# Spectral filter tail spread into block form by one masked VectorE product per block, with three copies moved to ScalarE and a new order of the filter stage

## The chip, the cores and the metric

The kernel runs on one core of a Trainium2 chip. The metric is the device time of one execution in microseconds (us); the profile's span is about 1.9 us shorter, because it runs from the first to the last instruction. Before the change the median was 494.26 us in three runs (493.99 to 494.33). All runs quoted here were in the fast state, with a granted TensorE clock of 1.0 (0.997 in one run of e5).

## The reference

Two layers over 2048 tokens of width 576: a spectral filter (two-dimensional real FFT, product with a learned complex filter, inverse FFT), then a gated feed-forward layer of width 4608, each after a layer norm and each added to its input.

```python
def _A_ref(x, w_r, w_i):
    X = jnp.fft.rfft2(x.astype(jnp.float32), axes=(-2, -1))
    return jnp.fft.irfft2(X * (w_r + 1j * w_i), s=(S, D), axes=(-2, -1)).astype(jnp.bfloat16)
def _B_ref(x, w_gate, w_up, w_down):
    return (_gelu(x @ w_gate) * (x @ w_up)) @ w_down
h  = x + _A_ref(_layernorm(x), A_w_r, A_w_i)
h2 = h + _B_ref(_layernorm(h), B_w_gate, B_w_up, B_w_down)
```

## The kernel before

The transforms are matmuls with tables. The middle of the first layer, the **filter stage**, works on 16 groups of frequencies and runs from about 20 to 51 us. Each group i passes through these steps, whose order is a hand-written list:

- D: matmuls into PSUM, copied to CUS; B: matmuls on CUS, copied to YS.
- T: VectorE multiplies YS by the filter weights WS (and their negated copy, made by the operations "w", the **flips**).
- Z: VectorE adds the halves: a wide part ZS (256 columns) and a narrow part ZR (the last 32 of 288 columns, the **tail**). Four groups share the 128 columns of one ZR block.
- V: matmuls on ZS, result copied to the array V. R: matmuls on a ZR block, result copied to VR.

The inverse transform then takes V and VR as 128-row operands. The four groups in a block of 128 rows must not mix, so VR is block-shaped: rows 32j to 32j+31 hold data only for group j and zeros for the other three. Before the change the zeros come from one fill and the data from one narrow copy per group. In the code, `P.op` records one operation of an engine with what it reads (r) and writes (w), `ev` a copy out of PSUM, and `bank(b, ...)` is a piece of PSUM bank b (abridged):

```python
def st_R(q, engs, b=7):
    # ... n = 32 columns per group of this block
    for zp in range(2):
        P.op(PE, lambda t, ...: t.matmul(bank(b, 0, n, 0, 256), ZR[:, q % 2, zp, 0:n], VT[:, sp_, zp, :], ...))
    for j, i in enumerate(js):
        ev(engs[j], VR[32*j:32*j+32, :, :, GORD[i], :]..., bank(b, 32*j, 32*j+32, 0, 256)..., [("PS", b), "Vz"], ...)

P.op(POOL, lambda g: g.memset(VR[:, :, :, :, :], 0.0), r=[("ATS", c) for c in range(NT)], w=["Vz"])
for w in SEQF:      # the order of the filter stage, a list of steps
    ...
```

`engs` says for each copy whether VectorE (DVE) or ScalarE (ACT) does it; another list, VENG, does so for the V copies. What follows is the inverse transform (I, N), the second norm and, from 62.34 us to the end, the feed-forward.

Of the kernel before, what the change touches and what calls it, by code (L numbers as in the profile page):

```python
# [5 lines left out]
F32 = mybir.dt.float32  # L6
ACTF = mybir.ActivationFunctionType
ALU = mybir.AluOpType
# [7 lines left out]
NT = 16  # L16
# [6 lines left out]
SEQ1 = """k14 B0 B1 v0 Q2 S2 B3 q0 v1 n0 n2 c0 q1 S4 x0D c1 M0 E1A B6 E0A Q4 B5 B7 x1P v2 E2D n1 B8 E3A E4A k104 M1 q2 c2 B9 Q10 E5A E7A n3 v3 S10 B12 E6A q3 c3 x2P B11 k202 M2 E9A x3P Q13 v4 E12A E8A q4 n4 B14 c4 B15 E10A E11A S13 E13D M3 E14A E15A v5 x4P E16D q5 E17A c5 E18A M4 n5 x5D E20D E19A E22D E21A M5 E23D E24A E25A E27A E26D E29A E28D""".split()  # L23
LORD = "x0-2 x2-4 a0-4 x4-8 a4-8 x8-12 x12-16 a8-16".split()
ACT_TILES = tuple(int(w[1:]) for w in SEQ1 if w[0] == "Q")
SEQF = """D0 w1 w0 D1 D2 B0 T0 B1 T1 Z1 D3 D4 B2 Z0 D5 T2 B3 T3 Z2 B4 T4 D6 B5 D7 Z3 B6 Z4 T5 T6 V0 V1 Z5 Z6 D8 R0 B7 D9 V2 T7 w3 D10 V3 Z7 w2 B8 T8 B9 V4 T9 Z9 B10 D11 R1 Z8 D12 T10 V5 D13 B11 Z10 B12 V6 D14 T11 T12 B13 Z11 V7 D15 Z12 T13 R2 B14 V8 Z13 B15 T14 V9 Z14 T15a V11 V12 T15b V10 V13 Z15a Z15b V14 V15 R4 R3""".split()
RENG = [['dve', 'dve', 'act', 'act'], ['act', 'dve', 'act', 'dve'], ['dve', 'dve', 'act', 'dve'], ['act', 'act', 'dve'], ['dve']]
VENG = [('act',), ('act',), ('act',), ('act',), ('act',), ('dve',), ('act',), ('act',), ('act',), ('act',), ('act',), ('act',), ('act',), ('act',), ('dve',), ('dve', 'act')]
DENG, BENG = ['act', 'dve', 'dve', 'act', 'act', 'act', 'act', 'act', 'act', 'act', 'act', 'act', 'act', 'act', 'act', 'act'], ['dve', 'act', 'act', 'act', 'act', 'act', 'act', 'act', 'act', 'act', 'act', 'act', 'act', 'act', 'act', 'act']
QR = ((0, 2), (2, 4), (4, NPRE), (NPRE, 16))  # L30
SEQ = """I0 I1 N0 I2 s0 N1 I3 N2 m0 s1 I4 r0 q0 s2 N3 c0 m1 s3 n1 n0 r1 I5 q1 N4 I6 A1 c1 n3 A0 n2 N5 I7 D2 z3 N6 N7""".split()
# [278 lines left out]
def _build(nc, A_x, A_w_r, A_w_i, B_w_gate, B_w_up, B_w_down, out):  # L310
    P = Prog(nc)
    T = build_tables()
    dram = {n: nc.inline_tensor(_np_bf16(T[n]), name="c_" + n.lower()) for n in T}
    PE, DVE, ACT, SP, POOL = "pe", "dve", "act", "sp", "pool"
# [3 lines left out]
    sb = SbufMap(nc, base, top)  # L318
# [11 lines left out]
    V = sb.alloc("V", [128, NT, 4, NG, 8], BF16)  # L330
    VR = sb.alloc("VR", [128, NT, 2, NG, 8], BF16)
# [22 lines left out]
    TM = sb.alloc("TM", [128, 2, NT], F32)  # L354
    RS2 = sb.alloc("RS2", [128, NT], F32)
    EPT = sb.alloc("EPT", [128, 1], F32)
    OS = sb.alloc("OS", [128, 2, D], BF16)
    shared = (sb.off + 63) // 64 * 64

# [12 lines left out]
    VT = sb.alloc("VT", [128, 2, 2, 256], BF16)  # L372
# [7 lines left out]
    ATS = sb.alloc("ATS", [128, NT, 128], BF16)  # L380
# [7 lines left out]
    ZR = sb.alloc("ZR", [128, 2, 2, 128], BF16)  # L388
# [8 lines left out]
    PS = nc.alloc_psum_tensor("PS", [128, 4096], F32)  # L397

    def bank(b, p0=0, p1=128, c0=0, c1=512):
        return PS[p0:p1, b * 512 + c0:b * 512 + c1]  # L400
# [4 lines left out]

    P.op(POOL, lambda g: g.memset(EPT[:, :], EPS), w=["EPT"])
    P.op(POOL, lambda g: g.memset(ZD[:, :], 0.0), w=["ZD"])
    xv = A_x[0].rearrange("(p c) d -> p c d", c=NT)
    ov = out[0].rearrange("(p c) d -> p c d", c=NT)
    tabs = dram["ATAB"].rearrange("p (c k) -> p c k", c=NT)  # L410
# [34 lines left out]
    GORD = list(range(1, NG)) + [0]  # L445
# [34 lines left out]
    def ln1_sqrt(i):  # L480
        c0, c1 = GROUPS[i]
        P.op(ACT, lambda a, c0=c0, c1=c1: a.activation(RS1[:, c0:c1], MV1[:, c0:c1, 1], ACTF.Sqrt, bias=EPT[:, 0:1]),
             r=[("MV1", c) for c in range(c0, c1)] + ["EPT"], w=[("SD1", i)])

# [56 lines left out]
    RUN1 = {"k": idle_mm, "S": act_sum, "Q": act_sq, "B": ln1_tile, "v": ln1_var, "q": ln1_sqrt, "c": ln1_rs, "M": a_mm, "x": ln1_scale, "E": a_ev, "n": x_neg}  # L541
    P.op(ACT, lambda a: a.activation(SA[:, 0, 0:1], EPT[:, 0:1], ACTF.Sqrt), r=["EPT"], w=[("SA0", 0)])
    for w in SEQ1:
        a = w[1:]
# [8 lines left out]
    FB, used = {}, [0] * 8  # L553
    for t, w in enumerate(SEQF):
        k, i = w[0], w[1:].rstrip("abc")
        if k in "DB":
            late = ("V", 0) in FB or any(x[0] == "V" for x in SEQF[t:t + 4])
            b = min((0, 2, 4) if late else (0, 2, 4, 6), key=lambda b: max(used[b], used[b + 1]))
            used[b] = used[b + 1] = t + 1
        elif k in "VR":  # L560
            b = min((6, 7) if ("D", LAST) not in FB else range(8), key=lambda b: used[b])
            used[b] = t + 1
            if k == "V":
                b2 = b
                if int(i) == LAST and len(VENG[LAST]) > 1:
                    b2 = min(range(8), key=lambda b: used[b])
                    used[b2] = t + 1
                b = (b, b2)
# [4 lines left out]
    def ev(eng, dst, src, r, w):  # L573
        fn = (lambda v: v.tensor_copy(dst, src)) if eng == DVE else (lambda a: a.activation(dst, src, ACTF.Copy))  # L574
        P.op(eng, fn, r=r, w=w)

    def st_D(i, eng=ACT):
        g = GORD[i]
        b0, s3 = FB["D", i], i % 3
        for o in range(2):  # L580
            b = b0 + o
            for m, us in enumerate((1 - o, 3 - o, 4) if o == 0 else (4, 1 - o, 3 - o)):
                P.op(PE, lambda t, b=b, m=m, us=us, o=o, g=g: t.matmul(bank(b, 0, 128, 0, 2 * HK), U[:, us, g, :, :], FT[:, 3 * o + (2 if us == 4 else us // 2), :], start=(m == 0), stop=(m == 2)),  # L583
                    r=uk[us] + ["FT"], w=[("PS", b)])
        ev(eng, CUS[:, s3, :, :].rearrange("p a (j r) -> p a j r", r=2), banks(b0, 2, 2 * HK).rearrange("p r (a j) -> p a j r", a=2),
           [("PS", b0), ("PS", b0 + 1)], [("CU", s3)])
# [18 lines left out]
    def st_w(i):  # L605
        for g0, g1 in (((1, 5),), ((5, 9),), ((9, 13),), ((13, 16), (0, 1)))[i]:
            P.op(DVE, lambda v, g0=g0, g1=g1: v.tensor_scalar(WS[:, 0, g0:g1, :], WS[:, 2, g0:g1, :], -1.0, None, op0=ALU.mult),  # L607
                 r=[k for k in (wkeys[0] if i < 2 else wkeys[1] if i < 3 else wkeys[0] + wkeys[1]) if k[2] == 1], w=[("Wn", 4 * i + k) for k in range(4)])
# [19 lines left out]
            ev(e, V[:, :, k0:k1, g, :].rearrange("p n k e -> p k n e"), bank(b[a], 0, 128, 128 * k0, 128 * k1).rearrange("p (k n e) -> p k n e", k=k1 - k0, n=16),  # L628
               [("PS", b[a])], [("V", g, k) for k in range(k0 // 2, k1 // 2)])

    def st_R(q, engs, b=7):
        js = [i for i in range(4 * q, 4 * q + 4) if i < LAST] if q < 4 else [LAST]
        sp_, n = (1, 32) if q == 4 else (0, 32 * len(js))
        for zp in range(2):
            P.op(PE, lambda t, b=b, zp=zp, n=n, q=q, sp_=sp_: t.matmul(bank(b, 0, n, 0, 256), ZR[:, q % 2, zp, 0:n], VT[:, sp_, zp, :], start=(zp == 0), stop=(zp == 1)),
                 r=[("ZR", q % 2, j) for j in range(len(js))] + ["VT"], w=[("PS", b)])
        for j, i in enumerate(js):
            ev(engs[j], VR[32 * j:32 * j + 32, :, :, GORD[i], :].rearrange("p n k e -> p k n e"), bank(b, 32 * j, 32 * j + 32, 0, 256).rearrange("p (k n e) -> p k n e", k=2, n=16),
               [("PS", b), "Vz"], [("V", GORD[i], 2)])

    def idle_ft(n, b):
        for _ in range(n):
            P.op(PE, lambda t, b=b: t.matmul(bank(b, 0, 128, 0, 2 * HK), FT[:, 0, 0:128], FT[:, 0, :], start=True, stop=True), r=["FT"], w=[("PS", b)])


    P.op(POOL, lambda g: g.memset(VR[:, :, :, :, :], 0.0), r=[("ATS", c) for c in range(NT)], w=["Vz"])
    for w in SEQF:
        i = int(w[1:].rstrip("abc"))
        if w[0] == "w":
            st_w(i)  # L650
        elif w[0] == "D":
            st_D(i, DENG[i])
        elif w[0] == "B":
            st_B(i, BENG[i])
        elif w[0] == "T":
            if w[-1] in "ab":
                st_T(i, *((0, 256, (0,)) if w[-1] == "a" else (256, KW, (1,))))
            else:
                st_T(i)
        elif w[0] == "Z":  # L660
            st_Z(i, {"a": (0,), "b": (1,)}.get(w[-1], (0, 1)))
        elif w[0] == "V":
            st_V(i, FB["V", i], VENG[i])
        elif w[0] == "R":
            st_R(i, RENG[i], FB["R", i])


    wdv = B_w_down[:, :].rearrange("(c p) d -> p c d", p=128)
# [14 lines left out]
    P.alias(["FT", "BT", "VT"], [("HT", 0, i, k) for i in range(4) for k in range(5)])  # L683

    vk = [[("V", g, c) for g in range(NG)] for c in range(3)]
    vkeys = vk[0] + vk[1] + vk[2] + ["Vz"]


    SLOT = {}
# [36 lines left out]
    def square(c, out, key):  # L726
        P.op(ACT, lambda a, c=c, out=out: a.activation(out, XO[:, c, 0:D], ACTF.Square, accum_out=SB2[:, 1, c:c + 1]),  # L727
             r=[("X", c)], w=[key, ("S1", c)])
# [26 lines left out]
    def ln2_q(q):  # L755
        c0, c1 = QR[q]
        P.op(ACT, lambda a, c0=c0, c1=c1: a.activation(RS2[:, c0:c1], RS2[:, c0:c1], ACTF.Sqrt, bias=EPT[:, 0:1]), r=[("V2", q), "EPT"], w=[("SD2", q)])

# [38 lines left out]
    def sq(c):  # L797
        square(c, OS[:, c % 2, :], ("OS", c % 2, 0))

# [75 lines left out]
    def down(tb, p):  # L875
# [3 lines left out]
        for h, (d0, d1) in enumerate(((0, cut), (cut, D))):  # L879
# [4 lines left out]
            for f in [*range(36)] if tb == 0 else [*range(9, 36), *range(9)]:  # L884
                if cd < NT and f == 22:
# [3 lines left out]
                     r=[("AT", f), ("WD", f // 4)], w=[("PS", b)])  # L889
            P.op(DVE, lambda v, b=b, d0=d0, d1=d1, p=p, c=c: v.tensor_tensor(OS[:, p % 2, d0:d1], bank(b, 0, 128, 0, d1 - d0), XO[:, c, d0:d1], op=ALU.add),  # L890
                 r=[("PS", b), ("X", c)], w=[("OS", p % 2, k) for k in (range(2) if d1 == cut and cut > 288 else (h,))])
            P.dma(SP, ov[:, c, d0:d1], OS[:, p % 2, d0:d1], f"so{p % 2}{h}", r=[("OS", p % 2, h)], w=[("OUT", p % 2, h)])

# [35 lines left out]
def bass_sequential_preLN__spectral_gfnet__geglu_ffn__prompt_kernel(  # L929
    nc, A_x, A_w_r, A_w_i, B_x, B_w_gate, B_w_up, B_w_down, out  # L930
):
    _build(nc, A_x, A_w_r, A_w_i, B_w_gate, B_w_up, B_w_down, out)
# [28 lines left out]
```

## Time and profile before

| What | Value | From |
|---|---|---|
| Time, span | 494.26 us, 492.4 us | runs, page |
| Filter stage | 20.2 to 50.7 us | chain of waits |
| Inverse transform and second norm | 50.7 to 62.3 us | chain of waits |
| Feed-forward | 62.3 to 490.1 us, TensorE without a gap | chain of waits |
| Narrow copies to VR | 9 on VectorE of 0.416 us, 7 on ScalarE of 0.372 us | groups by form |
| Zero fill of VR | 3.52 us on GpSimd | timeline |

The page's first line gives shares of the whole span, in which 428 us of feed-forward drown the 31 us that matter here. Such a stage is read from the chain of waits and from busy times by stretch; the prediction shows both.

### The profile page before, as it was taken

What the parts mean: (1) busy time and instruction counts of PE and PEld (TensorE: products, weight loads), DVE (VectorE), ACT (ScalarE), POOL (GpSimd) and SP (SyncE); (2) the same over time, 40 slices, a digit from 0 to 9 for tenths busy, and PEclk for the clock granted to TensorE, in tenths of its full rate; (3) what the DMA queues carried; (4) which work ended last, traced back from release to release, by engine and by line L of the source; (5) the groups of instructions that cost most, each with busy time, mean ns of one, the idle gap of its engine ahead of it and who ended that gap; (6) DMA issues with size and microseconds to landing.
All of it is one profiled execution on the core that took longest, in us unless ns stands there. A gap on an engine that the chain in (4) does not pass through costs nothing.

```text
span 492.4 us, 9854 instructions
## 1 busy us (share of the span) xinstructions
PE 485.6 (99%) x4338; PEld 288.9 (59%) x4338; DVE 196.1 (40%) x423; ACT 156.2 (32%) x300; POOL 27.7 (6%) x37
## 2 busy tenths in 40 slices
PE   7999999999999999999999999999999999999998
PEld 3787655555588844444577644444677544444775
DVE  6999734344455544433311043333211233333111
ACT  6799855233322143223200022322100132333000
POOL 5510701000000010000000000000000000000000
DMA  8990998311000071100000001000000000000000
GB/s 281 215 332 19 344 341 288 117 28 22 1 13 19 14 227 26 25 3 1 1 13 19 19 14 25 17 1 1 7 19 12 14 1 1 1 1 2 12 19 19
DMA packets 25147, 31.26 MB, mean 63 GB/s; under 512 B 11440, under 2 KB 17840, under 8 KB 25104
## 3 DMA queue, kind: packets, MB, share of 16 engines
q1 hardware_dynamic: 22208, 18.68, 13.6%
q0 software_dynamic: 2896, 11.95, 7.1%
q8 instruction: 34, 0.56, 0.5%
q14 instruction: 9, 0.07, 0.1%
HBM read 26.29 MB, written 2.36 MB: 58 GB/s over the span
## 4 chain that ended last, share of the span: by engine, by line
PE 90%; DVE 6%; ACT 1%; DMA 1%; issue 1%; SPq 0%; DVEq 0%
PE PS L837 57%; PE PS L887 29%; DVE ST L467 1%; DMA XO<-in_A_x_dram 1%; PE PS L583 1%; DVE TP L602 1%; PE PS L854 1%; PE PS L593 1%; DVE U L532 1%; PE PS L697 1%; PE PS L736 1%; DVE XO L739 0%; PE PS L868 0%; DVE ZS L613 0%; DVE WS L607 0%
## 5 line engine op out<-in xcount | busy, mean ns | idle before, releaser
L837 PE MATMUL PS<-HT,WG 64*128 64x512 bf16 x2106 | 228.5, 376 | 0.0
L837 PEld LDWEIGHTS PS<-HT,WG 64*128 64x128 bf16 x2106 | 107.6, 94 | 119.5 <-issue 1.0
L847 DVE TENSOR_TENSOR AT<-GL,PS 128x512 bf16<-128x512 bf16 x144 | 98.8, 687 | 175.0 <-ACT GL L846 175.0
L846 ACT ACTIVATE GL<-PS 128x512 bf16<-128x512 f32 x144 | 85.8, 597 | 257.3 <-PE PS L837 245.0
L887 PE MATMUL PS<-WD,AT 128*128 128x288 bf16 (+2 forms) x1152 | 144.2, 286 | 0.0
L887 PEld LDWEIGHTS PS<-WD,AT 128*128 128x128 bf16 x1152 | 110.8, 98 | 30.7 <-ACT GL L846 0.8
L890 DVE TENSOR_TENSOR OS<-PS,XO 128x288 bf16<-128x288 f32 (+2 forms) x32 | 14.6, 458 | 100.3 <-PE PS L887 100.3
L837 PE MATMUL PS<-HT,WGX 64*128 64x512 bf16 x486 | 53.4, 376 | 0.0
L837 PEld LDWEIGHTS PS<-HT,WGX 64*128 64x128 bf16 x486 | 23.7, 94 | 28.8
L727 ACT ACTIVATE JD<-XO 128x576 bf16<-128x576 bf16 x8 | 5.5, 683 | 28.5 <-DVE XO L871 28.5
L583 PE MATMUL PS<-FT,U 128*128 128x288 bf16 x96 | 14.1, 286 | 0.0
L602 DVE TENSOR_TENSOR TP<-YS,WS 128x1152 bf16<-128x1152 bf16 (+2 forms) x17 | 11.8, 721 | 1.0 <-ACT YS L574 0.5
L523 PE MATMUL PS<-ATS,XO 128*128 128x128 bf16 (+1 forms) x128 | 10.1, 221 | 1.2 <-POOL XN L537 0.7
L467 DVE BATCH_NORM_STATS2 ST<-XO 128x6 f32<-128x288 bf16 x24 | 9.3, 438 | 4.2 <-DMA XO<-in_A_x_dram 4.2
L583 PEld LDWEIGHTS PS<-FT,U 128*128 128x128 bf16 x96 | 9.2, 98 | 2.5 <-DVE U L532 0.2
L574 ACT ACTIVATE YS<-PS 128x576 bf16<-128x576 f32 x15 | 9.7, 662 | 2.5 <-PE PS L593 2.2
L593 PE MATMUL PS<-CUS,BT 128*128 128x288 bf16 x64 | 10.0, 286 | 0.2 <-DVE CUS L574 0.2
L770 DVE TENSOR_SCALAR HN<-XO,TM,RS 128x576 bf16<-128x576 bf16 (+1 forms) x32 | 10.0, 362 | 0.0
L523 PEld LDWEIGHTS PS<-ATS,XO 128*128 128x128 bf16 (+1 forms) x128 | 7.5, 97 | 4.1 <-POOL XN L537 1.2
L623 PE MATMUL PS<-VT,ZS 128*128 128x256 bf16 x64 | 8.8, 273 | 0.5 <-DVE ZS L613 0.5
L871 DVE SCALAR_TENSOR_TENSOR XO<-PS,XO 128x576 bf16<-128x576 f32 x8 | 6.1, 758 | 8.1 <-PE PS L868 8.1
L574 ACT ACTIVATE CUS<-PS 128x576 bf16<-128x576 f32 x14 | 9.1, 655 | 0.6 <-PE PS L583 0.4
(80 smaller groups left out, 217.0 us busy)
## 6 DMA issues: line engine op xcount, KB each, us to landing
WD<-in_B_w_down_dram POOLq DMA_DIRECT2D x9, 576.0 KB, 21.5
WG<-in_B_w_up_dram SPq DMA_DIRECT2D x4, 1152.0 KB, 8.7
WG<-in_B_w_gate_dram POOLq DMA_DIRECT2D x4, 1152.0 KB, 10.1
out_dram<-OS SPq DMA_DIRECT2D x30, 72.0 KB, 1.6
XO<-in_A_x_dram SPq DMA_DIRECT2D x3, 576.0 KB, 7.2
WGX<-in_B_w_gate_dram POOLq DMA_DIRECT2D x1, 1152.0 KB, 6.7
WGX<-in_B_w_up_dram SPq DMA_DIRECT2D x1, 1152.0 KB, 10.8
HT<-HN SPq DMA_TRANSPOSE x60, 2.4
```

The source lines that it names most:

```text
L467: P.op(DVE, lambda v, c=c, h=h: v.bn_stats(ST1[:, c, h, :], XO[:, c, 288 * h:288 * h + 288]), r=[("X", c)], w=[("ST1", c, h)])
L523: P.op(PE, lambda t, b=b, lhs=lhs, p0=p0, p1=p1, s=s, e=e, o=o, c=c: t.matmul(bank(b, p0, p1, o, o + 128), lhs, ATS[:, c, :], start=s, sto ...
L574: fn = (lambda v: v.tensor_copy(dst, src)) if eng == DVE else (lambda a: a.activation(dst, src, ACTF.Copy))
L583: P.op(PE, lambda t, b=b, m=m, us=us, o=o, g=g: t.matmul(bank(b, 0, 128, 0, 2 * HK), U[:, us, g, :, :], FT[:, 3 * o + (2 if us == 4 else u ...
L593: P.op(PE, lambda t, b=b, tb=tb, m=m, s3=s3, sp_=sp_: t.matmul(bank(b, 0, 128, 0, KW), BT[:, sp_, tb, :], CUS[:, s3, m, :], start=(m == 0) ...
L602: P.op(DVE, lambda v: v.tensor_tensor(TP[:, sl, :, :, q0:q1], y4, w4, op=ALU.mult), r=[("Y", sl), ("Wn", i)] + (wkeys[0] if 1 <= g < 9 els ...
L770: P.op(eng, lambda v, c=c, hs=hs, o0=o0, o1=o1, x0=x0, x1=x1: v.tensor_scalar(HN[:, hs, o0:o1], XO[:, c, x0:x1], TM[:, 1, c:c + 1], RS2[:, ...
L837: op = P.op(PE, lambda t, h0=h0, kt=kt, wt=wt, b=b, s=(not second and j == 0), e=(second and j == n - 1): t.matmul(bank(b), wg_tile(slot)[ ...
L846: P.op(ACT, lambda a: a.activation(GL[:, s2, :], bank(b0), ACTF.Gelu_apprx_tanh), r=[("PS", b0)], w=[("GL", s2)])
L847: P.op(DVE, lambda v: v.tensor_tensor(AT[:, f, :], GL[:, s2, :], bank(b0 + 1), op=ALU.mult), r=[("GL", s2), ("PS", b0 + 1)], w=[("AT", f)])
L887: P.op(PE, lambda t, b=b, d0=d0, d1=d1, f=f, p=p: t.matmul(bank(b, 0, 128, 0, d1 - d0), AT[:, f, 128 * p:128 * p + 128], WD[:, f, d0:d1], ...
L890: P.op(DVE, lambda v, b=b, d0=d0, d1=d1, p=p, c=c: v.tensor_tensor(OS[:, p % 2, d0:d1], bank(b, 0, 128, 0, d1 - d0), XO[:, c, d0:d1], op=A ...
```

## The change

One VectorE product per block replaces up to four narrow copies and the zero fill. It reads the 128 x 256 matmul result once for each group (a zero step in the access pattern) and multiplies it by a mask MK that is 1 where row block and group agree and 0 elsewhere. So it writes data and zeros together. Three V copies (V5, V14 and half of V15) move from VectorE to ScalarE, and the order of the stage is new.

```diff
-SEQF = """D0 w1 w0 D1 D2 B0 T0 B1 T1 Z1 D3 D4 B2 Z0 ... T15b V10 V13 Z15a Z15b V14 V15 R4 R3"""
-RENG = [['dve', 'dve', 'act', 'act'], ...]
-VENG = [... V5 ('dve',), ... V14 ('dve',), V15 ('dve', 'act')]
+SEQF = """w0 w1 D0 D1 D2 B0 T0 B1 T1 Z0 D3 B2 D4 B3 ... T15a Z15a V12 V14 Z15b R3 V15 R4"""
+VENG = [... all ('act',), V15 ('act', 'act')]
+    MK = sb.alloc("MK", [128, 4], F32)           # block mask, filled at the start
-            P.op(PE, ... bank(b, 0, n, 0, 256), ZR[:, q % 2, zp, 0:n], VT[:, sp_, zp, :] ...
-        for j, i in enumerate(js):
-            ev(engs[j], VR[32 * j:32 * j + 32, :, :, GORD[i], :] ...)
+            P.op(PE, ... bank(b, 0, 128, 0, 256), ZR[:, q % 2, zp, :], VT[...] reordered "p n k e" ...
+        P.op(DVE, lambda v: v.tensor_tensor(VR[:, :, :, g0:g0 + n, :]...,
+                  bank(b, 0, 128, 0, 256)....unsqueeze(2).to_broadcast([128, 32, n, 8]),
+                  MK[:, 0:n]....to_broadcast([128, 32, n, 8]), op=ALU.mult), r=[("PS", b), "MK"], ...)
-    P.op(POOL, lambda g: g.memset(VR[:, :, :, :, :], 0.0), r=[...], w=["Vz"])
```

(VENG, SEQF and the matmul lines are cut and abridged.)

More of the change, by code (lines that the diff above doesn't have):

```diff
@@ L25 @@
 ACT_TILES = tuple(int(w[1:]) for w in SEQ1 if w[0] == "Q")
-SEQF = """D0 w1 w0 D1 D2 B0 T0 B1 T1 Z1 D3 D4 B2 Z0 D5 T2 B3 T3 Z2 B4 T4 D6 B5 D7 Z3 B6 Z4 T5 T6 V0 V1 Z5 Z6 D8 R0 B7 D9 V2 T7 w3 D10 V3 Z7 w2 B8 T8 B9 V4 T9 Z9 B10 D11 R1 Z8 D12 T10 V5 D13 B11 Z10 B12 V6 D14 T11 T12 B13 Z11 V7 D15 Z12 T13 R2 B14 V8 Z13 B15 T14 V9 Z14 T15a V11 V12 T15b V10 V13 Z15a Z15b V14 V15 R4 R3""".split()
-RENG = [['dve', 'dve', 'act', 'act'], ['act', 'dve', 'act', 'dve'], ['dve', 'dve', 'act', 'dve'], ['act', 'act', 'dve'], ['dve']]
-VENG = [('act',), ('act',), ('act',), ('act',), ('act',), ('dve',), ('act',), ('act',), ('act',), ('act',), ('act',), ('act',), ('act',), ('act',), ('dve',), ('dve', 'act')]
+SEQF = """w0 w1 D0 D1 D2 B0 T0 B1 T1 Z0 D3 B2 D4 B3 D5 T2 Z1 B4 Z2 D6 T3 T4 V0 D7 B5 Z3 B6 w2 Z4 R0 T5 V1 D8 Z5 B7 T6 Z6 D9 B8 T7 V2 D10 V3 Z7 T8 Z8 D11 B9 R1 V5 B10 w3 T10 T9 D12 Z10 V4 D13 B11 Z9 T11 V6 B12 Z11 B13 T12 D14 T13 V8 Z13 D15 V7 Z12 B14 R2 B15 T14 V10 T15b V9 Z14 V11 V13 T15a Z15a V12 V14 Z15b R3 V15 R4""".split()
+VENG = [('act',), ('act',), ('act',), ('act',), ('act',), ('act',), ('act',), ('act',), ('act',), ('act',), ('act',), ('act',), ('act',), ('act',), ('act',), ('act', 'act')]
 DENG, BENG = ['act', 'dve', 'dve', 'act', 'act', 'act', 'act', 'act', 'act', 'act', 'act', 'act', 'act', 'act', 'act', 'act'], ['dve', 'act', 'act', 'act', 'act', 'act', 'act', 'act', 'act', 'act', 'act', 'act', 'act', 'act', 'act', 'act']
@@ L407, in _build @@
     P.op(POOL, lambda g: g.memset(ZD[:, :], 0.0), w=["ZD"])
+    P.op(POOL, lambda g: g.memset(MK[:, :], 0.0), w=["MK"])
+    for j in range(4):
+        P.op(POOL, lambda g, j=j: g.memset(MK[32 * j:32 * j + 32, j:j + 1], 1.0), w=["MK"])
     xv = A_x[0].rearrange("(p c) d -> p c d", c=NT)
@@ L629, in st_V, with st_R @@
                [("PS", b[a])], [("V", g, k) for k in range(k0 // 2, k1 // 2)])
-    def st_R(q, engs, b=7):
+    def st_R(q, b=7):
         js = [i for i in range(4 * q, 4 * q + 4) if i < LAST] if q < 4 else [LAST]
-        sp_, n = (1, 32) if q == 4 else (0, 32 * len(js))
+        sp_, g0, n = 1 if q == 4 else 0, GORD[js[0]], len(js)
         for zp in range(2):
-            P.op(PE, lambda t, b=b, zp=zp, n=n, q=q, sp_=sp_: t.matmul(bank(b, 0, n, 0, 256), ZR[:, q % 2, zp, 0:n], VT[:, sp_, zp, :], start=(zp == 0), stop=(zp == 1)),
-                 r=[("ZR", q % 2, j) for j in range(len(js))] + ["VT"], w=[("PS", b)])
-        for j, i in enumerate(js):
-            ev(engs[j], VR[32 * j:32 * j + 32, :, :, GORD[i], :].rearrange("p n k e -> p k n e"), bank(b, 32 * j, 32 * j + 32, 0, 256).rearrange("p (k n e) -> p k n e", k=2, n=16),
-               [("PS", b), "Vz"], [("V", GORD[i], 2)])
+            P.op(PE, lambda t, b=b, zp=zp, q=q, sp_=sp_: t.matmul(bank(b, 0, 128, 0, 256), ZR[:, q % 2, zp, :], VT[:, sp_, zp, :].rearrange("p (k n e) -> p n k e", k=2, n=16),
+                                                                  start=(zp == 0), stop=(zp == 1)),
+                 r=[("ZR", q % 2, j) for j in range(4)] + ["VT"], w=[("PS", b)])
+        P.op(DVE, lambda v: v.tensor_tensor(VR[:, :, :, g0:g0 + n, :].rearrange("p n k g e -> p (n k) g e"),
+                                            bank(b, 0, 128, 0, 256).rearrange("p (a e) -> p a e", e=8).unsqueeze(2).to_broadcast([128, 32, n, 8]),
+                                            MK[:, 0:n].unsqueeze(1).unsqueeze(3).to_broadcast([128, 32, n, 8]), op=ALU.mult),
+             r=[("PS", b), "MK"], w=[("V", GORD[i], 2) for i in js])
     def idle_ft(n, b):
@@ L643, in idle_ft @@
             P.op(PE, lambda t, b=b: t.matmul(bank(b, 0, 128, 0, 2 * HK), FT[:, 0, 0:128], FT[:, 0, :], start=True, stop=True), r=["FT"], w=[("PS", b)])
-    P.op(POOL, lambda g: g.memset(VR[:, :, :, :, :], 0.0), r=[("ATS", c) for c in range(NT)], w=["Vz"])
     for w in SEQF:
@@ L664, in _build @@
         elif w[0] == "R":
-            st_R(i, RENG[i], FB["R", i])
+            st_R(i, FB["R", i])
     wdv = B_w_down[:, :].rearrange("(c p) d -> p c d", p=128)
@@ L685, in _build @@
     vk = [[("V", g, c) for g in range(NG)] for c in range(3)]
-    vkeys = vk[0] + vk[1] + vk[2] + ["Vz"]
+    vkeys = vk[0] + vk[1] + vk[2]
     SLOT = {}
```

## The prediction

> **What bounds the kernel now.** I read the page's first part, then the chain of waits in order of time, then the busy time by stretch, then the timeline where the chain turned.
>
> ```profile
> PE 485.6 (99%) x4338; PEld 288.9 (59%) x4338; DVE 196.1 (40%) x423; ACT 156.2 (32%) x300; POOL 27.7 (6%) x37
> ```
>
> By this line TensorE is everything and VectorE has nothing to say. It is an average. The chain shows where that is false (columns: start us, us, what):
>
> ```profile
> 20.25 1.94 DVE WS L607 x2
> 22.19 0.67 DVE CUS L574
> 22.86 0.05 issue
> 22.91 0.66 PE PS L593 x4
> ...
> 48.61 0.61 PE PS L623 x4
> 49.22 0.69 PE PS L635 x4
> 49.90 0.02 issue
> 49.92 0.37 ACT VR L574
> 50.30 0.01 issue
> 50.31 0.38 ACT VR L574
> 50.69 0.05 issue
> 50.74 1.03 PE PS L697 x7
> ...
> 62.34 70.11 PE PS L837 x648
> ```
>
> From 62.34 on, the feed-forward part is one unbroken matmul stream (62.3 to 490 us) that the change does not touch. So all that the change can do is move the moment 62.34, through the filter stage that lies between 20 and 51. The chain passes twice through what is changed: at 20.25 the two sign-flip operations on the filter weights (WS), and at 49.92 the narrow copies of the tail (VR) that the inverse transform at 50.74 waits for. The stretches between:
>
> ```profile
> 31.00:36.00 5.00, 5.00 (x45) 4.11 (x42) 4.54 (x14) 4.94 (x11) 0.00 (x0) 1.00 1.04 344
> 36.00:41.00 5.00, 5.00 (x44) 3.94 (x42) 4.62 (x10) 4.98 (x11) 0.00 (x0) 1.00 0.23 79
> 41.00:46.00 5.00, 4.45 (x39) 3.54 (x38) 4.94 (x14) 4.78 (x11) 0.00 (x0) 1.00 0.00 0
> ```
>
> (Columns: stretch, length, then busy us of TensorE, weight loads, VectorE, ScalarE, GpSimd; clock; DMA.) Three engines are all at 90% or more; in the last row VectorE is the fullest. I take VectorE as the bound of the stage, with ScalarE close behind. TensorE is close too: 96+64+64+10 matmuls at about 0.12 and 0.11 us start to start make 27.6 us of the 30 from 19.66 to 49.85.
>
> And the place at 20.25 seen in the timeline, GpSimd and VectorE:
>
> ```profile
> 17.99 3.52 POOL L646 MEMSET VR<- 128x4096 bf16 x1 [0.84 <-DVE ATS L497]
> 20.17 1.65 DVE L607 TENSOR_SCALAR WS<-WS 128x1156 bf16<-128x1156 bf16 x1
> ```
>
> The zero fill of VR ends at 17.99+3.52 = 21.51. The weight flip that starts inside it takes 1.65 us and ends at 21.82; the same shape later takes 0.45 us. It ends 0.3 us after the fill does, as if it had waited for it.
>
> **What the Trainium skill says.** "SBUF — State Buffer", Who interferes with whom: VectorE's two-port modes and GpSimd share a port pair, the holder has it for its whole instruction and the other blocks fully. The trace agrees: 1.65 us against 0.45. "VectorE: DVE Perf Modes", The perf-mode tier table: a two-tensor operation with an operand in PSUM runs at one element per cycle; with the 0.96 GHz given there this is 1.04 ns per element. The trace agrees: copies from PSUM take 692 ns for 512 elements and 414 for 256, 1.09 ns each. "Perfetto Trace Analysis", Optimizing Scalar/DVE Operations: each instruction carries a fixed overhead, so fewer, larger ones help a saturated engine. The trace agrees here too, and this is what the change lives from, in the rows below: 32 partitions cost what 128 cost.
>
> ```profile
> L574 DVE CAST VR<-PS 32x256 bf16<-32x256 f32 x9 | 3.7, 416 | 0.1
> L574 DVE CAST V<-PS 128x512 bf16<-128x512 f32 x2 | 1.4, 692 | 0.1
> L574 DVE CAST V<-PS 128x256 bf16<-128x256 f32 x1 | 0.4, 414 | 0.0
> L574 ACT ACTIVATE VR<-PS 32x256 bf16<-32x256 f32 x7 | 2.6, 372 | 0.4 <-PE PS L635 0.3
> L847 DVE TENSOR_TENSOR AT<-GL,PS 128x512 bf16<-128x512 bf16 x144 | 98.8, 687 | 175.0 <-ACT GL L846 175.0
> ```
>
> **The change part by part.**
>
> Size of the new operation. The product spreads 256 columns to four groups: 1024 elements per partition, 768 for the block of three groups, 256 for the last. From the L847 row (same kind: two tensors, one in PSUM): 512/0.96 = 533 ns, so 154 ns fixed. That gives an estimate of 1.22, 0.95 and 0.42 us. In a full queue a VectorE operation starts about 0.07 us before its predecessor's record ends, so 1.15, 0.88 and 0.42 in the queue.
>
> Removed: 9 narrow copies on VectorE, 9 x 0.42 = 3.8 us; 7 on ScalarE, 7 x 0.375 = 2.6 us; the 3.52 us zero fill on GpSimd. Moved from VectorE to ScalarE: two V copies of 512 columns and one of 256, 1.6 us in the queue off VectorE, about 1.4 us onto ScalarE. Added on VectorE: 3 x 1.15 + 0.88 + 0.42 = 4.75 us. Five tiny fills of the mask early on GpSimd, which waits there for the first load anyway. Sum over the stage: VectorE -3.8 - 1.6 + 4.75 = -0.7 us; ScalarE -1.2 us. The matmul count stays; the tail matmuls become 128 wide, which does not change their 272 ns. The order of the stage is new as well, so I place the gains by stretch:
>
> 1. Head. Without the fill the two flips take about 0.4 us each and end near 21.0. The next VectorE operation, the copy of D1, then waits for its matmuls instead: the twelfth matmul of the stage starts near 21.2 and ends near 21.5. So it starts at 21.5, not 22.11: a gain of 0.6, not of the whole 1.2. TensorE's wait before 22.91 falls to nothing, 0.4 us. The first product T0 moves from 24.28 to about 23.7.
>
> 2. Body, T0 to the last wide Z (24.28 to 48.13 before, 23.85 us). VectorE loses 7 narrow copies and one V copy, 3.0 + 0.6, and gains three wide products, 3.45: 0.15 us less. ScalarE loses five narrow copies and gains a V copy, 1.4 us less. If VectorE is the bound and idles as much as before (about 1.3 us), the gain is 0.15.
>
> 3. Tail. Before, from the start of the last wide Z (48.13) to the inverse transform's first matmul on VR (50.74): 2.61 us. After, the listing of the program's order has behind that Z only its narrow part, the product of three groups and the product of one: 0.34 + 0.10 + 0.88 + 0.42 + 0.05 = 1.8 us. Gain 0.8. Both halves of the last V copy, on ScalarE, must fit into those 1.8 us: matmuls ready about 1.1 us after the Z starts, then 0.4, so they do.
>
> Sum: 0.6 + 0.15 + 0.8 = 1.55, I call it 1.6 us. 494.26 - 1.6 = **492.7 us**, 0.3%.
>
> **The rivals.**
>
> *The new order, not the operations, decides.* The streams of TensorE, VectorE and ScalarE in this stage are all rearranged; a wide product holds its PSUM bank for 1.2 us where the copies split between two engines held it 0.8, and the V blocks take turns on those banks. One added wait of 0.5 us per product would eat 1.5 us: time about 494. Against it: the order is made new with the change, VectorE's idle time of 1.3 us leaves as much to win as to lose, and ScalarE now has slack. If the order also wins back the idle time, 491.7.
>
> *TensorE becomes the bound.* From B1, about 22.5 after the head's gain, it has 27.6 less 22 x 0.122, 24.9 us of matmuls, and can't reach the inverse transform before 47.4. Against 50.7 less 1.6 this leaves 1.7 us, so it caps the gain near 3 us rather than denies it.
>
> *The wide product is slower than one element per cycle*, since it repeats each PSUM element four times and reads the mask with zero steps. Nothing in this trace shows such an access. At twice the time it adds 3.4 us to the body and 1.0 to the tail: the kernel would be near 497.
>
> *The start of the feed-forward is hidden anyway by a transfer.* Against it: in the chain the stretch 50.74 to 62.34 has no DMA in it, and the first gate weights are issued at 27.5 and land in 10 us by the page's median. So what VR gains should reach 62.34 whole.
>
> **Range and chances.** The three terms are each uncertain by 0.3 to 0.8 us, the body most. 80%: 491.7 to 493.8. Two per cent would be 9.9 us; no rival reaches that on either side, so the verdict is "same" with near certainty.
>
> **What would show each step.** In the profile after: the two flips at about 20.2 should take 0.45 us each with nothing of GpSimd beside them (else the head is wrong), and the copy of D1 should start near 21.5 after a wait on TensorE. The five products should be 1.2, 1.2, 1.2, 0.95 and 0.42 us (else the size rule is wrong). From the last wide Z to the first matmul on VR should be 1.8 us, and that matmul near 49.2. The feed-forward should start near 60.8 and take as long as before. The prediction is wrong if VectorE shows new idle time of over a microsecond waiting for ScalarE or TensorE in the body, or if what is gained by 50 us is lost again before 62.

## More of the kernel before

Chain of waits of the kernel before (start us, us, what):

```profile
33.45 0.54 ACT CUS L574
33.99 0.49 ACT V L574
...
36.15 0.52 DVE TP L602
```

For some microseconds ScalarE's copies carry the chain, then VectorE's products.

## The result, and the profile after

The changed kernel took 492.86 us (492.40 to 493.12, four runs) against 494.14 us for the kernel before. The ratio is 0.9973, with a 95% interval of 0.9956 to 0.999. A ratio is the mean time of one kernel's fast runs over that of the other's of the same rounds, so it is not quite the ratio of the medians quoted. It is a gain of 0.27%.

The copies' end of the profile first: the head of the stage (timeline of VectorE) and the new products (groups by form: count, then total us and mean ns), changed kernel:

```profile
20.14 0.82 DVE L610 TENSOR_SCALAR WS<-WS 128x1156 bf16<-128x1156 bf16 x2
21.47 1.49 DVE L577 CAST CUS<-PS 128x576 bf16<-128x576 f32 x2 [0.50 <-PE PS L586]
```

```profile
L641 DVE TENSOR_TENSOR VR<-PS,MK 128x1024 bf16<-128x1024 f32 x3 | 3.7, 1220 | 0.0
L641 DVE TENSOR_TENSOR VR<-PS,MK 128x768 bf16<-128x768 f32 x1 | 1.0, 951 | 0.0
L641 DVE TENSOR_TENSOR VR<-PS,MK 128x256 bf16<-128x256 f32 x1 | 0.4, 424 | 0.0
```

The two flips now take 0.82 us together, not 2.02, and VectorE then waits 0.50 us for TensorE, as predicted. The products cost what was estimated. The stretches that answer to those shown of before (length, then busy us of TensorE, weight loads, VectorE, ScalarE, GpSimd; clock; DMA):

```profile
31.00:36.00 5.00, 5.00 (x44) 4.12 (x43) 4.86 (x13) 4.73 (x9) 0.00 (x0) 1.00 0.76 256
36.00:41.00 5.00, 5.00 (x44) 4.06 (x43) 4.83 (x13) 4.95 (x10) 0.00 (x0) 1.00 0.02 7
41.00:46.00 5.00, 5.00 (x46) 4.29 (x45) 4.97 (x13) 4.99 (x10) 0.00 (x0) 1.00 0.00 0
```

TensorE now has no idle time in any of the three, where it had 0.55 us before. The same columns for the whole body, from the first product T0 to the last wide Z, before and then changed:

```profile
24.28:48.13 23.85, 23.27 (x195) 18.46 (x192) 22.67 (x58) 23.27 (x45) 1.51 (x2) 1.00 0.56 184
23.73:46.82 23.09, 23.09 (x198) 18.97 (x195) 22.57 (x53) 22.58 (x42) 1.51 (x2) 1.00 0.49 175
```

VectorE's busy time fell by only 0.10 us; what shrank is its idle time, from 1.18 to 0.52 us. The chain of waits of the changed kernel (asked up to 63 us) says the same and shows the tail:

```profile
44.14 1.32 PE PS L626 x12
...
45.52 0.22 DVE TP L605
...
46.82 0.43 DVE ZS L616
...
47.35 0.88 DVE VR L641
48.23 0.14 issue
48.36 1.63 PE PS L701 x12
...
53.03 0.77 DVE XO L743 x2
53.80 0.41 DVE TM L751
...
60.94 2.10 PE PS L841 x17
```

From 12.5 to 45.5 the chain is TensorE alone. At 47.35 it is the product of three groups, and the inverse transform's very first matmul waits for it. At 53.80 a small operation appears that was not on the chain at such a length before.

To compare runs I cut the time into four stretches at points that every profile has: the start of the first flip; the first product T0; the start of the last wide Z; the first inverse matmul that reads VR; the start of the feed-forward. That removes the first 20 us, where the start of the first flip wandered between 20.00 and 20.79 us over the 13 profiles. Within the stretches a kernel repeats: the changed kernel profiled twice gave 40.80 and 40.76 in sum; every other kernel was profiled once.

| Profile (us) | flip to T0 | T0 to last Z | last Z to VR | VR to feed-forward | sum |
|---|---|---|---|---|---|
| before | 4.11 | 23.85 | 2.61 | 11.60 | 42.17 |
| changed | 3.59 | 23.09 | 2.15 | 11.97 | 40.80 |
| e1 changed, fill put back | 4.12 | 22.96 | 2.15 | 11.97 | 41.20 |
| e2 before, fill early | 3.59 | 23.97 | 2.61 | 11.63 | 41.80 |
| e3 changed, old order | 3.59 | 23.19 | 2.69 | 11.55 | 41.02 |
| e4 before, new order | 4.12 | 23.72 | 2.89 | 11.97 | 42.70 |
| e5 changed, narrow products | 3.59 | 22.56 | 2.53 | 11.59 | 40.27 |
| e6 as e3, V copies not moved | 3.59 | 23.68 | 2.71 | 11.53 | 41.51 |
| e7 changed, other PSUM bank | 3.59 | 23.09 | 2.05 | 11.86 | 40.59 |
| e8 changed, loads by SyncE | 3.59 | 23.09 | 2.15 | 11.52 | 40.35 |
| e9 e7 and e8 together | 3.59 | 23.08 | 2.05 | 11.52 | 40.24 |
| e10 changed again | 3.58 | 23.09 | 2.15 | 11.94 | 40.76 |
| e11 before, V copies moved | 4.11 | 23.50 | 2.61 | 11.61 | 41.83 |

The change gives 0.52 + 0.76 + 0.46 us and takes 0.37 back: 1.37 us, which agrees with 0.27% of 494 us.

The expectations of e1 to e4 name absolute starts of the feed-forward. Counted from the first flip of the kernel that each run was made from, they came at 61.34, 61.97, 61.16 and 62.87 us. The last is just past the 62.8 that was expected at most.

### The profile page after: what moved, and what is told of

Its sections match the earlier page's. It is cut to its first block, busy times and chain, and to the rows that moved or that the text cites. A ratio compares the mean times of both kernels' runs of the same rounds, so it can differ in the third digit from the quotient of the medians.

```text
span 491.0 us, 9838 instructions
## 1 busy us (share of the span) xinstructions
PE 484.6 (99%) x4337; PEld 289.4 (59%) x4338; DVE 195.1 (40%) x416; ACT 155.5 (32%) x296; POOL 24.8 (5%) x41
## 4 chain that ended last, share of the span: by engine, by line
PE 95%; DVE 2%; DMA 1%; SPq 0%; issue 0%; POOL 0%; DVEq 0%; POOLq 0%
PE PS L841 57%; PE PS L891 29%; PE PS L586 2%; PE PS L596 2%; PE PS L526 1%; DMA XO<-in_A_x_dram 1%; PE PS L626 1%; PE PS L858 1%; PE PS L701 1%; PE PS L740 1%; DVE ST L470 1%; DVE XO L743 0%; PE PS L872 0%; SPq L219 0%; DVE HN L774 0%
```

## The experiments

Theory: VectorE, freed of the fill and of narrow copies, carries the gain. Rivals: the new order carries it, or other engines bind. Eleven runs were made (e10 is the changed kernel itself); in the three sessions the kernel before had a median of 494.35, 494.42 and 494.4 us.

**e1: the fill put back into the changed kernel.**

```diff
+    P.op(POOL, lambda g: g.memset(VR[:, :, :, :, :], 0.0), r=[("ATS", c) for c in range(NT)], w=["Vz"])
-             r=[("PS", b), "MK"], w=...
+             r=[("PS", b), "MK", "Vz"], w=...
```

> The changed kernel with the 3.52 us zero fill of VR put back on GpSimd where it was (the products wait for it; nothing else differs). Theory (port held by the fill): the first weight flip takes about 1.6 us again, the copy of D1 starts at 22.1 in place of 21.5, and since TensorE has no idle time afterwards, all that follows is 0.4 to 0.55 us later: feed-forward start near 61.4 (changed kernel 60.94), time 0.4 to 0.5 us longer. Rival (the stage absorbs it): feed-forward start within 0.1 us of 60.94.

Timeline of this run, GpSimd and VectorE:

```profile
17.82 3.52 POOL L651 MEMSET VR<- 128x4096 bf16 x1 [0.84 <-DVE ATS L500]
20.00 2.03 DVE L610 TENSOR_SCALAR WS<-WS 128x1156 bf16<-128x1156 bf16 x2
```

Without any other change the flips are back at 2.03 us. The stage is 0.40 us longer (41.20), as the theory had it. The time was 494.01 us, ratio 0.9994: more above the changed kernel (ratio 0.9969 in e10) than these 0.40 us explain, though the intervals overlap (0.9977 to 1.0011 against 0.9955 to 0.9982). The profiled run itself, with a span of 491.3 us against 491.0, fits the 0.40; what the other runs lost besides stays open.

**e2: the kernel before, with the fill alone moved to the start.**

```diff
+    P.op(POOL, lambda g: g.memset(VR[:, :, :, :, :], 0.0), w=["Vz"])      # right after the fill of U
-    P.op(POOL, lambda g: g.memset(VR[:, :, :, :, :], 0.0), r=[("ATS", c) for c in range(NT)], w=["Vz"])
```

> The kernel before, the fill alone moved to the start of the program, where GpSimd waits for the first load (3.3 to 6.8 us). Theory: the flips take 0.45 us each, D1 is copied from 21.5, and most of 0.55 us reaches the first matmul on VR (50.74 before): 50.2 to 50.4, feed-forward start near 61.9 (62.34 before). Rival (DVE in the body waits for other engines and swallows it): 62.3.

The flips took 0.82 us, T0 came 0.52 us earlier relative to the flip, and 0.37 us of that reached the feed-forward (41.80 against 42.17). The body gave 0.12 us back. So the fill's collision with the flips is worth 0.4 us in either kernel, and moving one line would have bought it without the product. The time was 494.04 us, ratio 0.9995, too close to tell by itself.

**e3: the changed kernel in the old order.** Edit: the changed kernel with the SEQF list of before.

> The changed kernel with the old order of the filter stage: operations, engines and missing fill as changed, the order as before. Theory of the prediction (the operations carry the gain, by 0.7 us less on VectorE and the head's 0.55): feed-forward start at 61.0 to 61.4, most of the 1.4 us gain. Rival (the new order carries it, wide products in the old order make TensorE and ScalarE wait): 61.8 or later, less than half of the gain.

The sum is 41.02 us: 1.15 of the 1.37 us, so the operations carry most and the rival falls. These operations include the three moved V copies, which e6 takes apart. Up to the first matmul on VR they give 1.10 us (29.47 against 30.57) and the order another 0.64; in the last stretch, which e8 explains, the new order loses 0.42 of that again. The body is 23.19, almost that of the changed kernel. What the new order brings is the tail: in the old order both last products stand at the end, behind TensorE (timeline of VectorE):

```profile
48.69 1.29 DVE L641 TENSOR_TENSOR VR<-PS,MK 128x256 bf16<-128x256 f32 x2 [0.82 <-PE PS L638]
```

VectorE waits 0.82 us for the tail's matmuls and then does 1.29 us on the path, 2.69 us for the stretch against 2.15. Time 493.36 us, ratio 0.9979.

**e4: the kernel before in the new order.** Edit: the kernel before with the new SEQF list.

> The kernel before with the new order of the filter stage alone: fill, narrow copies and their engines as before. Theory of the prediction: no gain, feed-forward start 62.2 to 62.8, since VectorE still has the same work and the fill still blocks the flip. Rival (order is the cause): 61.7 or earlier.

It is slower in the stretches, 42.70 us; the time, 494.98 us at a ratio of 1.0012 (0.9997 to 1.0027), is too close to tell by itself. The inverse transform waits for a V copy on VectorE (timeline of TensorE):

```profile
50.71 0.77 PE L697 MATMUL PS<-DT,V 128*128 128x288 bf16 x5 [0.51 <-DVE V L574]
```

The order alone gains nothing; it is made for the new operations.

**e5: what the products cost.** The first three products write one group in place of four.

```diff
+        if q < 3:
+            n = 1
```

with the fill of VR at the start as in e2, so that nothing is unwritten. The result is wrong; the comparison with the reference passed it all the same. So a pass there does not guard this part of the filter, and I take correctness of the block form from the code.

> The changed kernel with the first three wide products cut to one group each (256 elements in place of 1024; wrong result on purpose, the rest of VR is filled with zeros at the start of the program). Takes 3 x 0.8 = 2.4 us of VectorE out of the body (first product T to last wide Z, 23.09 us in the changed kernel). VectorE is the bound of the changed body: body 20.7 to 21.5 us. TensorE is its bound (the chain of the changed kernel says so): body 22.8 to 23.1 us and feed-forward start within 0.3 us of the changed kernel's, counted from the first weight flip.

2.4 us taken off VectorE shorten the body by 0.53 us, to 22.56. That fits neither figure exactly. It is much nearer to the second: four fifths of the time taken off VectorE were free. The feed-forward came 0.53 us earlier, not within 0.3, but not for that reason: 0.38 us of the body's gain is lost again before VR (2.53 against 2.15), and 0.38 us comes from the last stretch, which e8 explains. From 13.2 to 42.4 us the chain of waits of this run is TensorE alone; then, after 1.7 us of VectorE, it shows what stood next:

```profile
44.22 0.62 ACT YS L578
...
44.89 0.65 ACT YS L578
45.54 3.22 ACT V L578 x7
```

With VectorE out of the way, ScalarE's V copies bind the end of the stage. So this work of VectorE held the changed body up by half a microsecond. Time 493.15 us, ratio 0.9981, no shorter than the changed kernel's: the first flip began at 20.79 us in this run, the latest of all, and the chain of its first 13 us runs through GpSimd's fills at the start, the 3.53 us fill of VR among them. So here the early fill was not free; in e2, without the five fills of the mask before it, the chain does not touch it.

**e6: e3 with the V copies left where they were.** Edit: the VENG list of before.

> Old order, wide products, no fill, and the three V copies left on VectorE as before. Against the kernel before, in the body VectorE has 0.45 us more (three products of 1.15 for seven copies of 0.43) and ScalarE 1.9 us less (five narrow copies). VectorE is the bound of the old body: body 24.1 us or more (before 23.85). ScalarE was: body 23.4 us or less. In the tail V14, V15 and both products queue on VectorE: longer than in the run with the old order and moved V copies (2.69 us).

Body 23.68 us: between the two answers. VectorE had 0.45 us more than in the kernel before by the count of operations (0.33 by busy time in the body), and yet the body was 0.17 us shorter, and 0.29 shorter than in e2, where the fill is out of the way too. So what ScalarE shed (1.9 us by count, 1.19 by busy time) seems to count. No run takes work off ScalarE alone, so this is argued and not isolated. From e3 and e6 one can solve for two prices: VectorE's queue time at 1.1 us per us, ScalarE's at 0.35. Two runs fix two numbers, so this is an estimate to be tested, which e11 does. The tail was 2.71 us, hardly longer than in e3, so that part of the expectation failed. Time 493.69 us, ratio 0.9987.

**e7: another bank for the last block.**

```diff
-            st_R(i, FB["R", i])
+            st_R(i, 6 if i == 3 else FB["R", i])
```

> The changed kernel with the tail of groups 12 to 14 put in PSUM bank 6 in place of bank 0, which the inverse transform's first matmul takes next. Theory (a new wait: that matmul waits for the three-group product to free bank 0): from the last wide Z to the first matmul on VR 1.85 us in place of 2.15, feed-forward start 0.3 us earlier counted from the first flip. Rival (the wait is for the V copies or the last product all the same): no change, 2.1 us or more.

The first inverse matmul no longer waits for VectorE. Timeline of TensorE, the changed kernel, then this run:

```profile
48.36 0.77 PE L701 MATMUL PS<-DT,V 128*128 128x288 bf16 x5 [0.23 <-DVE VR L641]
```

```profile
48.68 0.77 PE L701 MATMUL PS<-DT,V 128*128 128x288 bf16 x5
```

The wait was real, but only 0.10 us of the hoped 0.3 came of it (2.05 against 2.15): right behind it stand TensorE's own last matmuls, four on ZS and two on ZR, and in this run the chain goes through them (47.72 to 48.55). Time 492.81 us, ratio 0.997.

**e8: the down-weight loads issued by SyncE.** In the changed kernel the first small operation on the second norm's sums (two elements per row) took 0.48 us. Timeline of VectorE, before, then changed:

```profile
55.50 0.17 DVE L747 TENSOR_SCALAR TM<-SB 128x2 f32<-128x2 f32 x1
```

```profile
53.72 0.48 DVE L751 TENSOR_SCALAR TM<-SB 128x2 f32<-128x2 f32 x1
```

GpSimd issues nine weight loads from 49.71 to 56.52 us in the changed kernel. The edit:

```diff
-        P.dma(POOL, WD[:, 4 * j:4 * j + 4, :], ...)
+        P.dma(SP, WD[:, 4 * j:4 * j + 4, :], ...)
```

> The changed kernel with the nine loads of the down weights issued by SyncE in place of GpSimd. Theory (the first small operation on the sums, 0.48 us in place of 0.17, waits for a port that GpSimd holds[...]): both such operations 0.17 us, from the first inverse matmul on VR to the feed-forward 11.5 to 11.6 us in place of 11.97, time 0.3 to 0.4 us shorter. Rival (chance, or the operation waits on something of VectorE's own): 0.48 us again.

Timeline of VectorE in this run:

```profile
53.97 0.16 DVE L751 TENSOR_SCALAR TM<-SB 128x2 f32<-128x2 f32 x1
```

The second such operation took 0.17 us. The last stretch is 11.52 us in place of 11.97. The cause is the issue of those loads by GpSimd. It is not the traffic: the DMA engines' busy share from 52 to 54 us was 1.05 in the changed kernel and 1.04 here. That the thing held is the shared port is the account of the Trainium skill ("SBUF — State Buffer", Who interferes with whom), which this run fits but does not isolate. In e7 the two operations happened to be short, and a scaling operation was hit instead: four of them took 1.52 us there and 1.18 here. So which operation pays depends on where the loads fall, and e10, the same program as the changed kernel, paid at the same place again (0.46). So did e1 and e4, which have the new order (0.48 each); e3 and e6 in the old order did not (0.17 and 0.16). Time 492.67 us, ratio 0.9965.

**e9: both edits.** Edit: e7 and e8 together.

> The two edits together on the changed kernel: tail of groups 12 to 14 in bank 6, down weights issued by SyncE. If the two gains add (0.1 us in the tail, 0.45 us between the inverse transform and the feed-forward), from the first flip to the feed-forward 40.2 to 40.3 us (changed kernel 40.80), and 0.3 to 0.6 us less than the changed kernel timed beside it. If they only trade places: 40.35 or more.

**e10: the changed kernel beside it, unedited.**

> The changed kernel itself once more, unedited, so that the run with both edits has it beside it on the same chip: 492.4 to 493.2 us, from the first flip to the feed-forward 40.8 us again, the first operation on the sums again 0.48 us if its wait is fixed by the program's order and not by chance.

The gains add: 40.24 us against 40.76. In five timed runs each on the same chip e9 took 492.47 us (492.22 to 492.65, ratio to before 0.996) and the changed kernel 492.84 us (492.57 to 493.18, ratio 0.9969). The ranges just overlap. It is the best version, 0.37 us below the changed kernel beside it; e8 alone, timed on another chip, was 0.20 us longer (492.67).

**e11: the kernel before with the three V copies moved.** Edit: the new VENG list in the kernel before.

> The kernel before with nothing changed but the engines of three V copies (V5, V14, first half of V15 from VectorE to ScalarE). In the body VectorE has 0.61 us less and ScalarE 0.5 more. Two runs fit as VectorE at full price and ScalarE at about a third: body 23.3 to 23.4 us (before 23.85). Rival (both engines bind alike, what one sheds the other takes): 23.7 to 23.9. Tail longer than 2.61 us, since ScalarE then has V14, both halves of V15 and two narrow copies in a row.

Body 23.50 us, 0.35 less than before. The fit from e3 and e6 asked for 0.45 to 0.55, the rival for at most 0.15. So unloading VectorE is worth more than loading ScalarE costs, but the prices are not constants; their size stays open. The tail did not grow (2.61), against the expectation. Time 493.99 us, ratio 0.999.

Laid in a row, the sums of the table split the gain of 1.37 us: 0.37 for the fill taken away from the flips (before to e2), 0.29 for the products in place of the narrow copies (e2 to e6), 0.49 for the three moved V copies (e6 to e3), 0.22 for the order (e3 to changed). The split depends on the order of the steps: the V copies alone gave 0.34 (e11). The product that gives the change its name is not its largest part.

## Why the prediction was right

The time was 0.16 us from the predicted 492.7 and inside the range. The stage gained 1.37 us where 1.55 was summed, but that closeness is partly luck: three terms were off by 0.3 to 0.6 us and cancelled.

- **Head** (0.6 predicted): right. The flips took 0.82 us together, and the copy of D1 came 1.33 us after the first flip in place of 1.94, behind a wait of 0.50 us on TensorE. T0 gained 0.52. e1 and e2 show it caused by the fill; 0.4 us of it arrives.
- **Size of the products** (1.22, 0.95 and 0.42): right, 1.220, 0.951 and 0.424. That is 1.04 ns more per element from 256 to 1024, the rate that the prediction had checked on copies only (1.09). The rival of a slower access falls.
- **Body** (0.15 predicted, 0.76 measured): mis-sized. The step that failed is "If VectorE is the bound and idles as much as before": it priced only VectorE's queue and counted the 1.4 us off ScalarE as nothing. VectorE's busy time fell by 0.10 us, near the count; its idle time did not stay but fell by 0.66. e6 points to ScalarE's relief as what did it (the body shortened although VectorE had more to do). e3 puts 0.66 of the 0.76 us on the operations and not the order.
- **Tail** (0.8 predicted, 0.46 measured): mis-sized. VectorE's work behind the last Z ended when predicted: the last product ended at 48.59, 1.77 us after that Z began, against 1.8. The step that failed was to look only at the first matmul that reads VR: five matmuls on V stand ahead of it in the queue, 0.61 us, and the first of them waited for PSUM bank 0, held by the three-group product (e7). Behind that stands the next wait, 0.1 us further.
- **"What VR gains should reach 62.34 whole"**: failed by 0.37 us. The prediction named this as what would prove it wrong. Shifting the stage made a small VectorE operation fall on GpSimd's issue of loads (e8).
- **Rivals**: the order is worth 0.22 us with the new operations (e3 against changed; 0.64 before the loss to the loads) and costs 0.53 us without them (e4). TensorE did become the bound of the body, as a cap: it has no idle time there, and e5 shows that four fifths of the 2.4 us taken off VectorE were free. The sign of being wrong that the prediction named, over a microsecond of new idle time of VectorE in the body, did not come: 0.52 us in all.

## What to carry to other kernels

Where three engines are each over 90% busy in a stage, price what a change takes off each of them, not only off the fullest: the chain of waits changes hands, and after the change the next engine caps the gain. On the path at a stage's end, follow the whole queue up to the first instruction that needs the data, including what waits for a buffer ahead of it. And look for fills and load issues on GpSimd beside VectorE's operations: moving a fill to an idle time and loads to another queue gave 0.4 us each here without touching the arithmetic.

## What the Trainium skill lacked or had wrong

- "SBUF — State Buffer", SBUF: two separate sides, tells of GpSimd-issued loads that wait for VectorE. The runs show the other direction as well: VectorE operations wait while GpSimd issues loads, 0.48 us in place of 0.16 for two elements per row, and 1.52 in place of 1.18 for four scaling operations; with the loads issued by SyncE it is gone. Who interferes with whom covers it by its general rule, but names load issue only as what has to wait, not as the holder.
- "VectorE: DVE Perf Modes", The TRN2 errata, gives (N+151)/0.96 ns for an fp32 two-tensor operation, in a section on SBUF sources. The runs show that it also holds with one operand in PSUM repeated by a zero step: 1220, 951 and 424 ns for 1024, 768 and 256 elements, against 1224, 957 and 424. The section's own row for PSUM sources, 120 cycles and one per element, would give 1192, 925 and 392, about 30 ns too little.
